# Storing two blocks to a transfer and asking for q and k two half-blocks sooner, in a fused attention and mixture-of-experts kernel

## The chip, the cores and the metric

The kernel runs on one core of a Trainium2 chip. The core has TensorE (PE, matrix products; PEld is its loading of weights), VectorE (DVE), ScalarE (ACT), GpSimd (POOL) and SyncE (SP), each with an instruction queue of its own that is worked through in order, and 16 DMA engines that all queues share. The metric is the device time of one execution in microseconds. The kernel before takes 1025.03 us (median of 3 runs, 1024.62 to 1025.8).

## The reference

Attention over 8 batches of 8 heads, 576 positions, head size 64, in a sliding window of 128 with a linear bias; its output, 4608 tokens by 512, goes through 8 experts that all tokens pass, weighted by a doubly normalised gate:

```python
scores = scale * np.matmul(q, k.transpose(0, 1, 3, 2))
scores = np.where(mask, scores + bias[None], -1000000000.0)
attn = softmax(scores)                       # written out in the reference
x = np.matmul(attn, v)  -> (4608, 512)
P = np.exp(x @ w_gate - max)
for _ in range(8):
    P /= P.sum(1, keepdims=True) + 1e-09
    P /= P.sum(0, keepdims=True) + 1e-09
    P *= N / E
for e in range(E):
    out += P[:, e:e + 1] * (np.maximum(x @ w1[e], 0.0) @ w2[e])
```

The gate P depends on sums over all tokens, so no expert's result can be weighted before the whole attention is done.

## The kernel before, in words

**Blocks and stages.** The tokens are 36 blocks of 128: four whole blocks of each batch (0 to 31), and the 64 last tokens of two batches together in each of blocks 32 to 35. The kernel has three stages: attention with experts 0 and 1 woven in (to about 285 us), the gate's eight rounds with the rest of experts 0 and 1 (to about 345 us), and experts 2 to 7 with a Strassen-like scheme (to the end).

**The attention loop.** `steps` goes over batch b, key block kb (0 to 4, the last one the 64-token tail) and half u of the heads; `at = 2 * kb + u` counts the ten half-blocks of a batch. A step does the scores and exponentials of the next half-block (`scores`, `exps`), its mask on VectorE (`masks`, L443), and the values product of this one (`values`, L468), whose normalised result VectorE writes into `xsb` (L479). Between them `filler.fill` puts in matmuls of experts 0 and 1 for blocks whose x is ready: `l1` (L115, ReLU on ScalarE L127) and `l2` (L137), whose result `psy` VectorE copies to a half-precision tile `yo` (`keep`, L555). `yo` is stored to DRAM (`ysp`, L541), since it can be weighted only after the gate. The order of blocks is 4 to 7 of expert 0, 0 to 3 of expert 1, 4 to 7 of expert 1, 8 to 11 of expert 0, 8 to 11 of expert 1, and so on. Blocks 0 to 3 of expert 0 go in one store of their own (L551).

**Buffers.** All PSUM products of this stage but the scores share four banks (`pmm`). `yo` is a ring of 6 tiles of one block, `xsb` one of 12, `a8` one of 8 large tiles for q, k, their casts `c16` and the turned `qk`. A tile that comes up again waits until its last use is over; for `yo` that is the landing of its store.

**SyncE's queue.** Every load, store and DMA transpose of the stage is issued by SyncE in the order in which the Python code emits it. `keep` calls `store(2)`, so that up to two older stores are held back and a block's store is emitted three copies later; `turn_x` likewise holds three of x's stores (`keep_x(3)`, L494). For batches from 3 on (`XPE = 3`) q and k go through: load (`load_qk`, L271), casts on VectorE and ScalarE (`cast_qk`, L287 and L289, at half-blocks 8, 9, 0 and 1), two DMA transposes (`turn_qk`, L301, at half-block 1), and a reordering on GpSimd for k and VectorE for q (`order_qk`, L312). x is turned by a DMA transpose too (`turn_x`, L519). At half-block 1 the tail of the next batch is loaded (`load_tail`, L260), and at every second half-block a block of v (`load_v`, L374). Where the step's calls stand:

```python
            if 1 <= b < B - 2 and at == 3:
                load_qk(b + 2)
            ...
                if at == 1:
                    turn_qk(b + 1)
                    order_qk(b + 1, 1, range(NDT))
```

**Last stage.** `yo`'s ring also serves the tiles `xtok`, `xs` and `s3` there; x is read back from `xd` and the results of experts 0 and 1 from `ysp`.

Of the kernel before, what the change touches and what calls it, by code (L numbers as in the profile page):

```python
# [14 lines left out]
def kernel(  # L15
# [10 lines left out]
    nc = tc.nc  # L26
# [137 lines left out]
            yield 0, a  # L164

    L1_US, L2_US = 0.87, 1.74
    XPE, YO, XSB = 3, 6, 12
    CAST_AT = ((0, 1, 2, 3), (1, 2, 3, 4))

    class Filler:  # L170
# [57 lines left out]
    sps = first_pool.enter_context(tc.tile_pool(name="sps", bufs=1, space=bass.MemoryType.PSUM))  # L228
    if True:
        mask = asb.tile([P, H, 2 * P], FP16, name="mask")  # L230
        rel = per.tile([P, HD], FP16, name="rel", tag="yo", bufs=YO)[:, 0 : 2 * P]

        def make_mask(ys):
            for y in ys:
# [80 lines left out]
                )  # L315

        def turn_tail(b):
            t16 = asb.tile([P, HD], FP16, name=f"t16_{b}", tag="xsb", bufs=XSB)
            nc.gpsimd.tensor_copy(out=t16, in_=tails.pop(b).rearrange("p h d -> p (h d)"))
            nc.sync.dma_start(out=QKT[b][2], in_=t16, transpose=True)  # L320

# [123 lines left out]
            )  # L445

        xsbs: dict = {}

        def values(b, kb, u):

            nk, _ = sizes(kb)
            if u == 0:
                xsbs[b, kb] = asb.tile([P, H, Dh], FP16, name=f"xsb_{b}_{kb}", tag="xsb", bufs=XSB)
            psN = aps.tile([P, GT], FP32, name=f"psN_{b}_{kb}_{u}", tag="pmm", bufs=4)
            if b == 0:
                spin(psN, 3)
            psN = psN[:, 0 : 4 * Dh + 4].rearrange("p (h d) -> p h d", h=4)
            ops = []
            for y in range(2):
                for hb in range(2):  # L460
                    hh = 2 * y + hb
                    if kb > 0:
                        ops.append((hh, pts[b, kb - 1, u][:, 2 * hb + y, P : P + nk], vs[b, kb - 1][:, 4 * u + hh, 0 : Dh + 1]))
                    ops.append((hh, pts[b, kb, u][0:nk, 2 * hb + y, 0:nk], vs[b, kb][0:nk, 4 * u + hh, 0 : Dh + 1]))
            if kb == NKB - 1:
                ops = ops[0::2] + ops[1::2]
            for i, (hh, lhsT, rhs) in enumerate(ops):
                nc.tensor.matmul(  # L468
                    out=psN[0:nk, hh, :],
                    lhsT=lhsT,  # L470
                    rhs=rhs,
                    start=(i == 0),
                    stop=(i == len(ops) - 1),
                )
# [15 lines left out]

        def keep_x(left=0):
            while len(kept) > left:
                blk, lo, nk, xsb = kept.pop(0)
                nc.sync.dma_start(out=xd[blk, lo : lo + nk, :], in_=xsb[0:nk].rearrange("p h d -> p (h d)"))  # L494

        def turn_x(b, kb):
            nk, _ = sizes(kb)
            blk = 4 * b + kb if kb < NKB - 1 else 4 * B + b // 2
            lo = 0 if kb < NKB - 1 else TL * (b % 2)
            xT, at = x_of(blk)  # L500
            to = xT[:, at, :, lo : lo + nk]
            xsb = xsbs.pop((b, kb))
            if by_pe(b):
                ps = aps.tile([P, NDT, P], FP16, name=f"psX_{b}_{kb}", tag="pmm", bufs=4)
                for j in range(NDT):
                    nc.tensor.matmul(
                        out=ps[:, j, 0:nk],
                        lhsT=xsb[0:nk, 2 * j : 2 * j + 2, :],
                        rhs=ident[0:nk, 0:nk],
                        is_transpose=True,  # L510
                        start=(j == 0),
                        stop=(j == NDT - 1),
                    )
                if b == 0:
                    nc.scalar.copy(out=to, in_=ps[:, :, 0:nk])
                else:
                    nc.vector.tensor_copy(out=to, in_=ps[:, :, 0:nk])  # L517
            else:
                nc.sync.dma_start(out=to, in_=xsb[0:nk].rearrange("p h d -> p (h d)"), transpose=True)  # L519
            kept.append((blk, lo, nk, xsb))  # L520
            keep_x(3)

        def gates(b0, b1):
            ps = aps.tile([P, b1 - b0, E], FP32, name=f"psG_{b0}", tag="pmm", bufs=4)
# [13 lines left out]
        def store(left=0):  # L538
            while len(stores) > left:
                e, blk, yo = stores.pop(0)  # L540
                nc.sync.dma_start(out=ysp[e, blk], in_=yo)  # L541

        first_y: list = []

        def keep(e, blk, ps):
            if blk < RI and e == 0:
                if not first_y:
                    first_y.append(per.tile([P, RI, HD], FP16, name="y_first", tag="a8", bufs=8))
                nc.vector.tensor_copy(out=first_y[0][:, blk, :], in_=ps)
                if blk == RI - 1:  # L550
                    nc.sync.dma_start(out=ysp[0, 0:RI].rearrange("m p d -> p m d"), in_=first_y[0])  # L551
                return
            store(2)
            yo = per.tile([P, HD], FP16, name=f"yo_{e}_{blk}", tag="yo", bufs=YO)
            nc.vector.tensor_copy(out=yo, in_=ps)  # L555
            stores.append((e, blk, yo))

        order = [(0, 0, 2), (0, 2, 2)]
        for b0 in range(RI, NBLK, 4):
# [129 lines left out]
        for n, (b, kb, u) in enumerate(steps):  # L689
# [72 lines left out]
                homes(1)  # L762
            if (b, at) == (1, 3):
                homes(2)
            if 1 <= b < B - 2 and at == 3:
                load_qk(b + 2)
            if XPE <= b + 1 < B - 1 and at >= 8:
                cast_qk(b + 2, at - 8)
# [113 lines left out]
        def scale_x(n):  # L882
            if n >= N:
                return
            g, e = units[n]
            for m in range(2):
                blk = 2 * g + m
                nc.scalar.mul(out=xs[2 * (n % 2) + m], in_=xtok[m], mul=P_sb[:, blk, e : e + 1])  # L888
            if e == E - 1 and n + 1 < N:
                if g == groups[0]:  # L890
                    xtok[:] = [per.tile([P, HD], FP16, name=f"xtok_{i}", tag="yo", bufs=YO) for i in range(2)]
                load_x(units[n + 1][0])

        def turn_xs(n):
# [19 lines left out]
        def quads_w1(e):  # L914
            w = W1L[e]
            q = dict(a11=w[:, 0:2, 0:HF], a12=w[:, 2:4, 0:HF], a21=w[:, 0:2, HF:Fd], a22=w[:, 2:4, HF:Fd])
            if e < E - 2:
                t = lp.tile([P, 3, 2, HF], FP16, name=f"s_{e}")
                q.update(s1=t[:, 0], s2=t[:, 1], s3=t[:, 2])
            elif e == E - 1:  # L920
                t = per.tile([P, 2, 2, HF], FP16, name=f"s_{e}", tag="xT", bufs=4)
                q.update(s1=t[:, 0], s2=t[:, 1])
                q["s3"] = [per.tile([P, HF], FP16, name=f"s3_{k}", tag="yo", bufs=YO) for k in range(2)]
            else:
                q.update((f"s{i}", aux[:, i].rearrange("p f n -> p (f n)").rearrange("p (k f) -> p k f", k=2)) for i in (1, 2, 3))
            q["s4"] = q["a21"]
            SL[e] = q

            def one(to, a, b, op):
                if isinstance(q[to], list):  # L930
                    for k in range(2):
                        nc.vector.tensor_tensor(out=q[to][k], in0=q[a][:, k], in1=q[b][:, k], op=op)
                else:
                    nc.vector.tensor_tensor(out=q[to], in0=q[a], in1=q[b], op=op)

            one("s1", "a21", "a22", ALU.add)
            one("s3", "a11", "a21", ALU.subtract)
            one("s2", "s1", "a11", ALU.subtract)
            one("s4", "a12", "s2", ALU.subtract)
# [28 lines left out]
        def part(n, ps, w, x, start=False):  # L968

            q = SL[units[n][1]][w]  # L970
            q = q if isinstance(q, list) else [q[:, k] for k in range(2)]
            for j in range(NF2):
                for k in range(2):
                    nc.tensor.matmul(  # L974
                        out=ps[:, j, :],
                        lhsT=q[k][:, P * j : P * j + P],
                        rhs=xset[n % 2][:, x, P * k : P * k + P],
                        start=(start and j == 0 and k == 0),
                        stop=(k == 1),
                        skip_group_check=True,  # L980
                    )
# [117 lines left out]
        s5 = s5y[:, 0].rearrange("p (f t) -> p f t", f=NF2)  # L1099
        y = s5y[:, 1].bitcast(FP16).rearrange("p (m d) -> p m d", m=2)  # L1100
        turn_xs(1)
        xs[:] = [per.tile([P, HD], FP16, name=f"xs_{i}", tag="yo", bufs=YO) for i in range(2)] * 2
        late: tuple = ()
        for n in range(N):
            g = units[n - 1][0]
# [103 lines left out]
```

## Time and profile before

| | |
|---|---|
| median of 3 runs | 1025.03 us (1024.62 to 1025.8) |
| profiled execution | 1025.63 us, span 1023.9 us |
| stores ysp<-yo | 68 of 128 KB, median 3.3 us to landing, 1.7 to 9.0 |
| stores xd<-xsb | 32 of 128 KB and 8 of 64 KB, median 3.2 us over both |
| q and k from batch 3 on | five loads each of 1024 KB, median 7.8 and 10.1 us |
| transposes qk<-c | ten, median 4.7 us |

Times on a timeline are microseconds from the span's start; a row gives start, duration, engine (SPq is SyncE's queue), line of the kernel, operation, output and inputs, count, and in brackets the idle time of the engine before it with what ended it. A transfer's row on SPq is the time that its issue held the queue; its landing is told apart from it.

### The profile page before, as it was taken

What the parts mean: (1) busy time and instruction counts of PE and PEld (TensorE: products, weight loads), DVE (VectorE), ACT (ScalarE), POOL (GpSimd) and SP (SyncE); (2) the same over time, 40 slices, a digit from 0 to 9 for tenths busy, and PEclk for the clock granted to TensorE, in tenths of its full rate; (3) what the DMA queues carried; (4) which work ended last, traced back from release to release, by engine and by line L of the source; (5) the groups of instructions that cost most, each with busy time, mean ns of one, the idle gap of its engine ahead of it and who ended that gap; (6) DMA issues with size and microseconds to landing.
All of it is one profiled execution on the core that took longest, in us unless ns stands there. A gap on an engine that the chain in (4) does not pass through costs nothing.

```text
span 1023.9 us, 27787 instructions
## 1 busy us (share of the span) xinstructions
PE 1000.3 (98%) x11487; PEld 801.6 (78%) x11487; DVE 749.5 (73%) x1594; ACT 722.2 (71%) x1240; POOL 78.8 (8%) x143
## 2 busy tenths in 40 slices
PE   7999999999999999999999999999999999999998
PEld 5645444444544698999999999999999999999997
DVE  5735665556578588877877877877887887787787
ACT  7646555555433457888888888888888888888885
POOL 1212033306110000000000000000000000000000
PEclk9999999999999999999999999999999999999999
DMA  9996689889999233343334334324334434333461
GB/s 244 219 271 170 143 221 220 191 196 180 221 192 177 69 72 80 71 81 94 74 64 100 76 66 94 73 64 94 77 65 98 81 71 81 86 82 65 98 115 47
DMA packets 264431, 122.46 MB, mean 120 GB/s; under 512 B 201968, under 2 KB 255728, under 8 KB 264304
## 3 DMA queue, kind: packets, MB, share of 16 engines
q1 hardware_dynamic: 249568, 102.68, 44.2%
q0 software_dynamic: 14304, 17.84, 10.5%
q8 instruction: 90, 1.47, 0.6%
q14 instruction: 37, 0.30, 0.1%
q10 hardware_dynamic: 432, 0.16, 0.1%
HBM read 78.30 MB, written 23.59 MB: 100 GB/s over the span
## 4 chain that ended last, share of the span: by engine, by line
PE 74%; DVE 3%; DMA 1%; ACT 1%; issue 0%; DVEq 0%; ACTq 0%; SPq 0%
PE psM L1011 30%; PE psB L974 13%; PE psA L974 9%; PE psC L974 9%; PE psy L137 5%; PE psh L115 5%; PE psh L953 2%; DVE acc L1055 1%; PE psN L468 1%; DMA acc<-xd 0%; DVE hs L1141 0%; PE psS L412 0%; DVE hs L991 0%; DVE hs L992 0%; DMA s5y<-ysp 0%
## 5 line engine op out<-in xcount | busy, mean ns | idle before, releaser
L1011 PEld LDWEIGHTS <-hs 128*128 128x128 f16 x2996 | 271.7, 98 | 22.4
L1011 PE MATMUL psM<-w2l,hs 128*128 128x256 f16 x1440 | 186.6, 273 | 0.0
L974 PEld LDWEIGHTS <-w1l 128*128 128x128 f16 x2720 | 173.2, 98 | 8.9 <-issue 3.0
L127 ACT ACTIVATE hT<-psh 128x512 f16<-128x512 f32 (+1 forms) x144 | 83.3, 586 | 100.9 <-PE psh L115 100.2
L987 ACT ACTIVATE hs<-hs 128x512 f16<-128x512 f16 x204 | 125.0, 630 | 34.3 <-DVE hs L1141 34.1
L1141 DVE TENSOR_TENSOR hs<-psB,s5y 128x512 f16<-128x512 f32 x102 | 70.4, 690 | 103.7 <-ACT xs L888 95.9
L115 PE MATMUL psh<-xT,w1t 128*128 128x512 f16 (+1 forms) x608 | 139.8, 368 | 3.2 <-DVE xT L517 2.4
L974 PEld LDWEIGHTS <-s 128*128 128x128 f16 x2040 | 135.3, 98 | 5.8
L888 ACT ACTIVATE xs<-xtok,L_sb 128x512 f16<-128x512 f16 x204 | 136.0, 720 | 0.6 <-DMA xset<-xs 0.6
L137 PE MATMUL psy<-w2t,hT 128*128 128x512 f16 x576 | 134.3, 379 | 0.0
L1011 PE MATMUL psM<-more,hs 128*128 128x256 f16 x864 | 129.0, 273 | 0.0
L974 PE MATMUL psA<-xset,w1l 128*128 128x128 f16 x1360 | 103.7, 219 | 0.0
L974 PE MATMUL psB<-xset,s 128*128 128x128 f16 x1360 | 103.7, 219 | 0.0
L137 PEld LDWEIGHTS <-hT 128*128 128x128 f16 x576 | 53.5, 98 | 60.9 <-issue 1.5
L555 DVE CAST yo<-psy 128x512 f16<-128x512 f32 x68 | 46.8, 690 | 72.1 <-PE psy L137 57.8
L115 PEld LDWEIGHTS <-w1t 128*128 128x128 f16 x608 | 54.7, 98 | 54.7 <-issue 7.0
L991 DVE TENSOR_TENSOR hs<-hs 128x1024 f16<-128x1024 f16 x107 | 74.0, 691 | 23.5 <-ACT hs L987 16.8
L430 ACT ACTIVATE pt<-psS 128x1024 f16<-128x1024 f32 (+2 forms) x80 | 67.7, 851 | 29.2 <-PE psS L412 22.7
L1135 ACT COPY psC<-psB 128x512 f32<-128x512 f32 x102 | 58.1, 570 | 36.5 <-PE psB L974 36.5
L1130 ACT COPY s5y<-psC 128x512 f32<-128x512 f32 x102 | 59.8, 586 | 25.5 <-PE psC L974 25.5
L443 DVE TENSOR_TENSOR pt<-pt,mask 128x1024 f16<-128x1024 f16 (+2 forms) x80 | 51.8, 647 | 32.8 <-ACT pt L430 32.7
L1055 DVE TENSOR_TENSOR acc<-acc,psM 128x256 f32<-128x256 f32 (+1 forms) x162 | 74.1, 503 | 2.1
(121 smaller groups left out, 1410.1 us busy)
## 6 DMA issues: line engine op xcount, KB each, us to landing
s5y<-ysp SPq DMA_DIRECT2D x36, 256.0 KB, 3.0
ysp<-yo SPq DMA_DIRECT2D x68, 128.0 KB, 3.3
v<-in_v_dram SPq DMA_DIRECT2D x32, 256.0 KB, 4.4
out_dram<-acc SPq DMA_DIRECT2D x31, 256.0 KB, 2.5
q<-in_q_dram SPq DMA_DIRECT2D x5, 1024.0 KB, 7.8
k<-in_k_dram SPq DMA_DIRECT2D x5, 1024.0 KB, 10.1
xtok<-xd SPq DMA_DIRECT2D x34, 128.0 KB, 2.3
w2t<-in_moe_w_dram POOLq DMA_DIRECT2D x4, 1024.0 KB, 10.9
```

The source lines that it names most:

```text
L115: nc.tensor.matmul(out=ps[:, 0:nt], lhsT=w1ts[e][:, dt, P * ft : P * ft + P], rhs=xT[:, at : at + nb, dt, :], start=(dt == 0), stop=(dt == ...
L127: nc.scalar.activation(out=st["hT"][:, ft, 0:nt], in_=ps[:, 0:nt], func=AF.Relu)
L137: nc.tensor.matmul(out=ps, lhsT=st["hT"][:, ft, P * ms : P * ms + P], rhs=w2ts[e][:, ft, :], start=(ft == 0), stop=(ft == NFT - 1),)
L430: nc.scalar.activation(out=pt[0:nk, :, 0 : nk + nn], in_=ps[0:nk, :, :, 0 : nk + nn].rearrange("p a y n -> p (a y) n"), func=AF.Exp, scale ...
L888: nc.scalar.mul(out=xs[2 * (n % 2) + m], in_=xtok[m], mul=P_sb[:, blk, e : e + 1])
L974: nc.tensor.matmul(out=ps[:, j, :], lhsT=q[k][:, P * j : P * j + P], rhs=xset[n % 2][:, x, P * k : P * k + P], start=(start and j == 0 and ...
L987: nc.scalar.activation(out=h[n][:, slot], in_=src, func=AF.Relu)
L991: nc.vector.tensor_tensor(out=t[:, 4:6], in0=t[:, 0:2], in1=t[:, 2:4], op=ALU.add)
L1011: nc.tensor.matmul(out=Ms[bk][:, half, :], lhsT=h[n][:, LEFT[m], f, :], rhs=W2L[e][RIGHT[m]][:, f, :], start=(e == 2 and f == 0 and half = ...
L1055: nc.vector.tensor_tensor(out=a, in0=a, in1=p2, op=op)
L1130: nc.scalar.copy(out=s5, in_=pc)
L1141: nc.vector.tensor_tensor(out=h[n][:, 3], in0=pb, in1=s5, op=ALU.add)
```

## The change

`yo` becomes a ring of 3 tiles of two blocks, `xsb` one of 6 tiles of two blocks, and a transfer to DRAM takes both blocks; the odd tail block of x still goes alone. A pair's store is emitted when the next pair is full (`store(1)` after the second copy). `load_qk(b + 2)` moves from half-block 3 to half-block 1 for b = 2 to 5, and there it stands in the code ahead of the casts and `turn_qk` of the same step. The tiles of the last stage that share the ring are cut from pairs, and the subtraction for s3 of the last expert is one instruction instead of two.

```diff
-    XPE, YO, XSB = 3, 6, 12
+    XPE, YO, XSB = 3, 3, 6
...
-            if u == 0:
-                xsbs[b, kb] = asb.tile([P, H, Dh], FP16, name=f"xsb_{b}_{kb}", tag="xsb", bufs=XSB)
+            if u == 0 and kb % 2 == 0:
+                pair = asb.tile([P, 2, H, Dh], FP16, name=f"xsb_{b}_{kb}", tag="xsb", bufs=XSB)
+                xsbs[b, kb], xsbs[b, kb + 1] = pair[:, 0], pair[:, 1]
+                pairs[b, kb] = pair
...
-                blk, lo, nk, xsb = kept.pop(0)
-                nc.sync.dma_start(out=xd[blk, lo : lo + nk, :], in_=xsb[0:nk].rearrange("p h d -> p (h d)"))
+                blk, lo, nk, n, pair = kept.pop(0)
+                nc.sync.dma_start(
+                    out=xd[blk : blk + n, lo : lo + nk, :].rearrange("m p d -> p m d"),
+                    in_=pair[0:nk, 0:n].rearrange("p m h d -> p m (h d)"),
+                )
...
-            kept.append((blk, lo, nk, xsb))
-            keep_x(3)
+            if kb % 2:
+                kept.append((blk - 1, lo, nk, 2, pairs.pop((b, kb - 1))))
+            elif kb == NKB - 1:
+                kept.append((blk, lo, nk, 1, pairs.pop((b, kb))))
+            keep_x(1)
...
-                nc.sync.dma_start(out=ysp[e, blk], in_=yo)
+                nc.sync.dma_start(out=ysp[e, blk : blk + 2].rearrange("m p d -> p m d"), in_=yo)
...
-            store(2)
-            yo = per.tile([P, HD], FP16, name=f"yo_{e}_{blk}", tag="yo", bufs=YO)
-            nc.vector.tensor_copy(out=yo, in_=ps)
-            stores.append((e, blk, yo))
+            if blk % 2 == 0:
+                yos.append(per.tile([P, 2, HD], FP16, name=f"yo_{e}_{blk}", tag="yo", bufs=YO))
+            yo = yos[-1]
+            nc.vector.tensor_copy(out=yo[:, blk % 2, :], in_=ps)
+            if blk % 2:
+                store(1)
+                stores.append((e, blk - 1, yo))
...
-            if 1 <= b < B - 2 and at == 3:
+            if 1 <= b < B - 2 and at == (3 if b == 1 else 1):
                 load_qk(b + 2)
...
-                q["s3"] = [per.tile([P, HF], FP16, name=f"s3_{k}", tag="yo", bufs=YO) for k in range(2)]
+                q["s3"] = per.tile([P, 2, HF], FP16, name="s3_e", tag="yo", bufs=YO)
```

More of the change, by code (lines that the diff above doesn't have):

```diff
@@ L230 @@
         mask = asb.tile([P, H, 2 * P], FP16, name="mask")
-        rel = per.tile([P, HD], FP16, name="rel", tag="yo", bufs=YO)[:, 0 : 2 * P]
+        rel = per.tile([P, 2, HD], FP16, name="rel", tag="yo", bufs=YO)[:, 0, 0 : 2 * P]
         def make_mask(ys):
@@ L317, in turn_tail @@
         def turn_tail(b):
-            t16 = asb.tile([P, HD], FP16, name=f"t16_{b}", tag="xsb", bufs=XSB)
+            t16 = asb.tile([P, 2, HD], FP16, name=f"t16_{b}", tag="xsb", bufs=XSB)[:, 0]
             nc.gpsimd.tensor_copy(out=t16, in_=tails.pop(b).rearrange("p h d -> p (h d)"))
@@ L447 @@
         xsbs: dict = {}
+        pairs: dict = {}
         def values(b, kb, u):
             nk, _ = sizes(kb)
-            if u == 0:
-                xsbs[b, kb] = asb.tile([P, H, Dh], FP16, name=f"xsb_{b}_{kb}", tag="xsb", bufs=XSB)
+            if u == 0 and kb % 2 == 0:
+                pair = asb.tile([P, 2, H, Dh], FP16, name=f"xsb_{b}_{kb}", tag="xsb", bufs=XSB)
+                xsbs[b, kb], xsbs[b, kb + 1] = pair[:, 0], pair[:, 1]
+                pairs[b, kb] = pair
             psN = aps.tile([P, GT], FP32, name=f"psN_{b}_{kb}_{u}", tag="pmm", bufs=4)
@@ L540, in store @@
                 e, blk, yo = stores.pop(0)
-                nc.sync.dma_start(out=ysp[e, blk], in_=yo)
+                nc.sync.dma_start(out=ysp[e, blk : blk + 2].rearrange("m p d -> p m d"), in_=yo)
         first_y: list = []
+        yos: list = []
         def keep(e, blk, ps):
@@ L890, in scale_x @@
                 if g == groups[0]:
-                    xtok[:] = [per.tile([P, HD], FP16, name=f"xtok_{i}", tag="yo", bufs=YO) for i in range(2)]
+                    t = per.tile([P, 2, HD], FP16, name="xtok", tag="yo", bufs=YO)
+                    xtok[:] = [t[:, 0], t[:, 1]]
                 load_x(units[n + 1][0])
@@ L929, in one @@
             def one(to, a, b, op):
[L930 to L934, printed above, removed]
+                nc.vector.tensor_tensor(out=q[to], in0=q[a], in1=q[b], op=op)
             one("s1", "a21", "a22", ALU.add)
@@ L970, in part @@
             q = SL[units[n][1]][w]
-            q = q if isinstance(q, list) else [q[:, k] for k in range(2)]
             for j in range(NF2):
@@ L975, in part @@
                         out=ps[:, j, :],
-                        lhsT=q[k][:, P * j : P * j + P],
+                        lhsT=q[:, k, P * j : P * j + P],
                         rhs=xset[n % 2][:, x, P * k : P * k + P],
@@ L1101 @@
         turn_xs(1)
-        xs[:] = [per.tile([P, HD], FP16, name=f"xs_{i}", tag="yo", bufs=YO) for i in range(2)] * 2
+        t = per.tile([P, 2, HD], FP16, name="xs", tag="yo", bufs=YO)
+        xs[:] = [t[:, 0], t[:, 1]] * 2
         late: tuple = ()
```

## The prediction

> **What bounds the kernel now.** I read the page first, then who waited for whom on TensorE, VectorE and ScalarE in the attention stage (75 to 350 us), then the timelines of SyncE, VectorE and TensorE round one batch.
>
> ```profile
> span 1023.9 us, 27787 instructions
> PE 1000.3 (98%) x11487; PEld 801.6 (78%) x11487; DVE 749.5 (73%) x1594; ACT 722.2 (71%) x1240; POOL 78.8 (8%) x143
> DMA  9996689889999233343334334324334434333461
> ```
>
> TensorE is the bound, and the DMA engines are nearly full for the first third only. The changed transfers lie there, so I look for TensorE's idle time there. The three next fences are waits from 75 to 350 us on TensorE and ScalarE, and from 60 to 345 on VectorE (total, times, longest).
>
> ```profile
> PE psN L468 <- DVE pt L443: 3.8, 4, 1.7
> PE psh L115 <- DVE xT L517: 1.4, 1, 1.4
> ```
> ```profile
> ACT c L289 <- DMA k<-in_k_dram: 14.7, 4, 7.3
> ```
> ```profile
> DVE yo L555 <- DMA ysp<-yo: 11.7, 5, 3.2
> ```
>
> TensorE's waits for VectorE sum to 5.2 us: no gain in this stage can be much more. Behind them stand two late transfers: k of the batch after next, for which ScalarE stood still 14.7 us, and stores of results, whose buffer a copy wants again, 11.7 us of VectorE. SyncE's queue in batch 3 (from 106.8 us on) shows why:
>
> ```profile
> 118.64 1.22 SPq L519 DMA_TRANSPOSE xT<-xsb  x1
> 119.92 1.42 SPq L494 DMA_DIRECT2D xd<-xsb  x1
> 121.39 0.42 SPq L374 DMA_DIRECT2D v<-in_v_dram  x1
> 121.91 6.18 SPq L301 DMA_TRANSPOSE qk<-c  x2
> 128.15 0.64 SPq L260 DMA_DIRECT2D t<-in_q_dram  x1
> 128.84 0.62 SPq L260 DMA_DIRECT2D t<-in_k_dram  x1
> 129.50 1.10 SPq L541 DMA_DIRECT2D ysp<-yo  x2
> ...
> 133.07 2.25 SPq L271 DMA_DIRECT2D q<-in_q_dram  x1
> 135.37 0.58 SPq L271 DMA_DIRECT2D k<-in_k_dram  x1
> 135.99 0.83 SPq L541 DMA_DIRECT2D ysp<-yo  x1
> ```
> ```profile
> q<-in_q_dram SPq DMA_DIRECT2D x1, 1024.0 KB, 7.7
> k<-in_k_dram SPq DMA_DIRECT2D x1, 1024.0 KB, 8.3
> ...
> ysp<-yo SPq DMA_DIRECT2D x1, 128.0 KB, 8.1
> ```
>
> The second fence has the landings of 133 to 137 us. k lands at 135.4 + 8.3 = 143.7 and the store issued behind it at 144.1, where such a store elsewhere takes 3.3 (median): what stands behind q and k in this queue lands after them. q to k took 10.6, 10.8 and 10.7 us in batches 3, 4 and 5. VectorE and TensorE at the two places that matter:
>
> ```profile
> 121.27 0.69 DVE L555 CAST yo<-psy 128x512 f16<-128x512 f32 x1 [0.70 <-PE psy L137]
> ...
> 125.85 0.69 DVE L555 CAST yo<-psy 128x512 f16<-128x512 f32 x1 [0.63 <-PE psy L137]
> ...
> 126.56 0.68 DVE L443 TENSOR_TENSOR pt<-pt,mask 128x1024 f16<-128x1024 f16 x1
> ...
> 144.16 0.69 DVE L555 CAST yo<-psy 128x512 f16<-128x512 f32 x1 [2.89 <-DMA ysp<-yo]
> ```
> ```profile
> 130.30 0.41 PE L468 MATMUL psN<-v,pt 128*128 128x65 f16 x8
> ```
>
> At 144.16 a copy stands until the store issued at 135.99 has landed; TensorE lost 1.7 us behind it and behind ScalarE's wait for k. The copies at 121.27 and 125.85 are blocks 9 and 10 of expert 0 (the copies counted in the program's order). The mask of 126.56 is what the values matmul of 130.30 needs.
>
> **What the change does, part by part.**
>
> *Fewer transfers.* 68 stores of results become 34, 40 of x become 24, so 50 issues go at 0.43 (ysp) and 0.58 us (xd): about 24 us of SyncE's time, which no one waits for except through a late transfer. Bytes stay. From 250 us on these stores are followed by nothing that the queue holds them for, and a copy comes 10 us and more after its buffer's store has landed; there the pairs cost nothing. A pair lands 256 KB; the nearest rows, `out` at 2.5 and `ysp` at 3.3 us, bound it, and I take 3. By the Trainium skill (DMA: Bandwidth & Descriptors, "Anatomy of one DMA") a transfer costs a fixed 2 us plus its bytes at 436 GB/s, which makes a pair 0.3 us later than a single; its fit is for the other kind of queue, and the sum would change by that 0.3 us at each wait below.
>
> *The rings of buffers.* Six singles become three pairs. Before, the store of a block was put in the queue three copies later and was due three copies after that. Now pair n goes into the queue after the second copy of pair n+1, and the first copy of pair n+3 waits for it: one pair's time is left, not counting what stands between in the queue. That is the step that I expect to cost. x's pairs (six of two for twelve) are reused a batch and a half later, long landed. In the last part the two subtractions for s3 become one, once, on VectorE beside TensorE: nothing.
>
> *q and k sooner.* In the built program of the changed kernel q and k now stand ahead of the transposes qk<-c of the same step, two half-blocks (6.5 to 11 us) sooner. ScalarE's and VectorE's waits for them go. But the transposes, the tail loads and the next store of results now stand behind 2 MB.
>
> *Batch 2* (gain). q and k move into a stretch where SyncE sits idle (76.9 to 85.9 us), so what stood behind them lands sooner; the 1.4 us (psh waiting for xT at 108 us, behind ScalarE's wait for k) go: -1.4, at worst 0.
>
> *Batch 3* (the main cost). The new order is xT, v, q, k, qk<-c twice, t twice, then the store of blocks 4 and 5 of expert 1, for which the copy of block 10 of expert 0 (125.85) waits. xT still waits for xsb, so q is issued at 118.64 + 1.22 + 0.5 = 120.4. k lands 10.6 later, 131.0. The transposes then need their own turn: two of them landed 2.5 us apart in batches 4 to 6, so 136. From the second transpose's landing to that of the store behind the tail loads took 2.3 us (batches 4 and 5): 138.3. The copy is held from 125.85 to 138.3, 12.4 us of VectorE, and in VectorE's queue behind it stand the logits' copy and the mask. The mask ended 1.4 us after the copy began (125.85 to 127.24), so now at 139.7; TensorE, which reached that matmul at 130.30, waits 9.4 us. What it can do till then without VectorE, it has done by 130.30. Less the 0.5 us that it waited at 132.1 anyway: +9. Lower bound: the transfers pass beside q and k and the store lands at 132.5 as now; then the mask is done at 133.9: +3.1 with that gap taken off. Upper: 139.5 with SyncE itself held up, +10.1. I take 9, because the row behind q and k at 135.99 shows the full delay.
>
> *End of batch 3.* The copy at 144.16 (block 10 of expert 1, ready at 141.3) then needs the pair (0: 8, 9), which stands behind xT<-xsb of the last full block (xsb done 140.64), xd, v: 140.6 + 1.2 + 0.6 + 0.5 + 2.5 and its issue = 145.5 on the old clock, against 144.07. That wait does not go, it changes its cause: +1.1 (0 to 1.5).
>
> *Batches 4 and 5.* The same step, but the copy that waits comes later (block 14 of expert 0, 163.91, for pair (1: 8, 9)). xT<-xsb at 150.0, q at 151.8, k lands 162.4, transposes 164.9 and 167.4, then t, xT, xd, v (4 us of issue from 165) and the store at 168.8: landed 171.7, 7.8 us of VectorE. TensorE has filler matmuls and one free PSUM bank until about 169 to 170, and the copy frees its bank at 172.4: +3 (0 if the transposes pass; 4.5 if the mask behind the copy is needed too). Later in these batches the second copy of a pair no longer waits (181.99, 2.07 us): TensorE's 1.3 us at 183 and 0.3 at 217 go. Batch 4: +1.7. Batch 5: +2.7.
>
> *Batch 6* loads no q or k; the store due at 233.4 lands near 237, TensorE loses 0.5 (0 to 1.5).
>
> Sum: -1.4 + 9 + 1.1 + 1.7 + 2.7 + 0.5 = +13.6 us. The profiled execution took 1025.63 (span 1023.9 and 1.7 round it), 0.6 over the median of the runs, 1025.03. So 1039.2 on its own time, and 1038.6 as a median.
>
> **Rivals.**
>
> *Relief* (faster). If pair stores land before the next pair's copy, the 50 issues less and the early q and k take the late transfers away: all of the 5.2 us go, 1025.0 - 5.2 = 1019.8, down to 1022 if half stays. For it: every one of the five store waits lies right behind a q and k load or in the backlog after one. Against it: the store that batch 3 needs is issued, even now, at 129.50, 3.6 us after the copy that will wait for it; it decides if the store lands before 128.9, which is 130.30 less the 1.4 us to the mask's end. The Trainium skill speaks for this case (DMA: Bandwidth & Descriptors, "Rules for kernel authors"): many small transfers are to be coalesced into one large one. No wait in this trace is for SyncE's issue time alone.
>
> *Transfers pass.* The wait in batch 3 is real, but the transposes and stores share the engines with q and k: +3.1 in batch 3, nothing in 4 to 6, the gains -1.4, -1.3, -0.3: 1025.1, up to 1030 where they pass only in part. Against it the 144.1 above.
>
> *Late transposes bite further.* kN (POOL) starts after the second transpose, now 5 to 6 us later, ahead of v's and the tail's casts, for which tT and the stores behind it wait in SyncE's queue: 4.5 in each of batches 4 and 5, 1 more at each one's end, 10.1 + 1.5 in batch 3, 1.5 in batch 6, no gains: +24.1, 1049.
>
> **How the numbers follow.** The main case 0.62 (own range 1031 to 1046), relief 0.13, transfers pass 0.16, the further bite 0.09. Within 0.2% (2 us, about what a measurement of this kernel can tell from no change) lies half of the third case: same 0.08. Faster 0.13, slower 0.62 + 0.08 + 0.09 = 0.79. The range 1025 to 1046 leaves out relief (0.13) and most of the last case (0.07).
>
> **What would show it.** Right: in waits, DVE yo L566 <- DMA ysp<-yo grows from 11.7 to 25 us and more, one of them near 12 in batch 3 round 126 to 138; TensorE's wait for the mask grows from 1.7 to about 9 there; ACT c <- DMA k is gone; qk<-c lands 8 us and more after issue. Wrong: that copy runs without a wait, because q and k drain faster than 10.6 us, or the transposes land beside them. Past 350 us both traces should differ by a constant.

## The result and the profile after

The changed kernel takes 1051.73 us (median of 4 runs, 1051.13 to 1053.71), the kernel before 1024.82 us in runs beside it: a ratio of 1.0264, 95% interval 1.0247 to 1.028, slower by 26.9 us. The profiled execution took 1051.13 us, 25.5 more than that of before. The first lines of its page, with the granted clock of the 40 slices (before: 9 in all of them):

```profile
span 1049.4 us, 27689 instructions
...
PE 1009.3 (96%) x11487; PEld 805.3 (77%) x11487; DVE 746.9 (71%) x1593; ACT 722.5 (69%) x1240; POOL 75.7 (7%) x143
...
PEclk8999989989999999999999999999999999999999
```

The same number of matmuls takes 9 us more of busy time, and TensorE stands idle longer: two losses, not one. The waits of TensorE (75 to 350 us) and VectorE (60 to 345 us), as total, times, longest:

```profile
PE psN L471 <- DVE yo L566: 15.2, 3, 6.9
PE psy L137 <- DVE yo L566: 2.2, 1, 2.2
PE psN L471 <- DVE pt L443: 2.2, 3, 1.2
PE psh L115 <- DVE xT L523: 1.4, 1, 1.4
```
```profile
DVE yo L566 <- DMA ysp<-yo: 34.3, 4, 12.3
```

VectorE's waits for stores grew from 11.7 to 34.3 us, and TensorE now waits behind the waiting copy. ScalarE's wait for k is gone after 75 us. SyncE's queue in batch 3, then VectorE and TensorE there:

```profile
120.99 1.23 SPq L525 DMA_TRANSPOSE xT<-xsb  x1
122.27 0.58 SPq L374 DMA_DIRECT2D v<-in_v_dram  x1
122.90 0.83 SPq L271 DMA_DIRECT2D q<-in_q_dram  x1
123.78 0.66 SPq L271 DMA_DIRECT2D k<-in_k_dram  x1
124.53 10.32 SPq L301 DMA_TRANSPOSE qk<-c  x2
134.90 1.01 SPq L260 DMA_DIRECT2D t<-in_q_dram  x1
135.97 0.63 SPq L260 DMA_DIRECT2D t<-in_k_dram  x1
136.64 0.62 SPq L550 DMA_DIRECT2D ysp<-yo  x1
```
```profile
126.32 0.69 DVE L443 TENSOR_TENSOR pt<-pt,mask 128x1024 f16<-128x1024 f16 x1 [0.87 <-ACT pt L430]
...
139.86 0.69 DVE L566 CAST yo<-psy 128x512 f16<-128x512 f32 x1 [12.29 <-DMA ysp<-yo]
...
140.56 1.41 DVE L443 TENSOR_TENSOR pt<-pt,mask 128x1024 f16<-128x1024 f16 x1
```
```profile
131.82 1.89 PE L137 MATMUL psy<-w2t,hT 128*128 128x512 f16 x8 [0.24 <-ACT hT L127]
140.60 0.21 PE L471 MATMUL psN<-v,pt 128*128 128x65 f16 x1 [6.89 <-DVE yo L566]
142.03 0.57 PE L471 MATMUL psN<-v,pt 128*128 128x65 f16 x7 [1.22 <-DVE pt L443]
...
144.55 3.60 PE L115 MATMUL psh<-xT,w1t 128*128 128x512 f16 x8
```

The order, the long issue and the late store are the ones forecast: the store is issued at 136.64, lands at 139.7, and the copy starts at 139.86. The last line is what the forecast did not have: eight matmuls take 3.60 us. Their row in the kernel before:

```profile
132.32 1.89 PE L115 MATMUL psh<-xT,w1t 128*128 128x512 f16 x8
```

The clock says why. Stretches of the kernel after: length, busy time of PE, PEld, DVE, ACT and POOL, then the granted clock, the DMA share and GB/s:

```profile
137.80:148.00 10.20, 6.18 (x28) 2.48 (x27) 6.54 (x14) 2.00 (x3) 6.20 (x9) 0.50 0.70 124
148.00:158.00 10.00, 10.00 (x77) 4.93 (x77) 6.33 (x16) 5.19 (x9) 1.32 (x4) 1.00 0.50 118
185.60:189.00 3.40, 3.40 (x10) 1.03 (x7) 3.33 (x9) 1.46 (x3) 0.51 (x2) 0.50 0.26 87
223.10:229.90 6.80, 4.40 (x17) 1.73 (x17) 5.47 (x12) 0.77 (x2) 2.81 (x8) 0.50 0.50 130
```

After each of the three long stalls TensorE runs at half of its clock. In batches 4 and 5 the stall and the slow matmuls behind it are these, the first row being that of twelve such matmuls in the kernel before:

```profile
168.86 2.75 PE L115 MATMUL psh<-xT,w1t 128*128 128x512 f16 x12
```
```profile
184.15 0.19 PE L471 MATMUL psN<-v,pt 128*128 128x65 f16 x1 [3.72 <-DVE yo L566]
...
184.85 4.44 PE L115 MATMUL psh<-xT,w1t 128*128 128x512 f16 x12
```
```profile
224.82 0.21 PE L471 MATMUL psN<-v,pt 128*128 128x65 f16 x1 [4.60 <-DVE yo L566]
...
226.09 4.65 PE L115 MATMUL psh<-xT,w1t 128*128 128x512 f16 x12
```

### The profile page after: what moved, and what is told of

It is laid out like the page before. It is cut to its first block, busy times and chain, and to the rows that moved or that the text cites. A ratio compares the mean times of both kernels' runs of the same rounds, so it can differ in the third digit from the quotient of the medians.

```text
span 1049.4 us, 27689 instructions
## 1 busy us (share of the span) xinstructions
PE 1009.3 (96%) x11487; PEld 805.3 (77%) x11487; DVE 746.9 (71%) x1593; ACT 722.5 (69%) x1240; POOL 75.7 (7%) x143
## 3 DMA queue, kind: packets, MB, share of 16 engines
q0 software_dynamic: 14304, 17.84, 10.2%
## 4 chain that ended last, share of the span: by engine, by line
PE 85%; DVE 5%; issue 4%; DMA 4%; SPq 1%; ACT 1%; POOL 0%; DVEq 0%; POOLq 0%; ACTq 0%
PE psM L1020 30%; PE psB L983 13%; PE psh L115 10%; PE psy L137 9%; PE psA L983 8%; PE psC L983 8%; PE psh L963 2%; DMA ysp<-yo 1%; PE psN L471 1%; PE psS L412 1%; DMA v<-in_v_dram 1%; DVE pt L443 1%; PE psT L351 1%; SPq L301 1%; DMA k<-in_k_dram 1%
## 5 line engine op out<-in xcount | busy, mean ns | idle before, releaser
L115 PE MATMUL psh<-xT,w1t 128*128 128x512 f16 (+1 forms) x608 | 145.8, 380 | 3.3 <-DVE xT L523 2.4
L137 PE MATMUL psy<-w2t,hT 128*128 128x512 f16 x576 | 134.3, 379 | 2.4 <-DVE yo L566 2.2
L983 PEld LDWEIGHTS <-s 128*128 128x128 f16 x1904 | 126.3, 98 | 5.6 <-issue 0.2
L983 PE MATMUL psB<-xset,s 128*128 128x128 f16 x1224 | 93.3, 219 | 0.0
## 6 DMA issues: line engine op xcount, KB each, us to landing
w2t<-in_moe_w_dram POOLq DMA_DIRECT2D x4, 1024.0 KB, 11.1
```

The costliest lines, as they stand in the source:

```text
L115: nc.tensor.matmul(out=ps[:, 0:nt], lhsT=w1ts[e][:, dt, P * ft : P * ft + P], rhs=xT[:, at : at + nb, dt, :], start=(dt == 0), stop=(dt == ...
L137: nc.tensor.matmul(out=ps, lhsT=st["hT"][:, ft, P * ms : P * ms + P], rhs=w2ts[e][:, ft, :], start=(ft == 0), stop=(ft == NFT - 1),)
L983: nc.tensor.matmul(out=ps[:, j, :], lhsT=q[:, k, P * j : P * j + P], rhs=xset[n % 2][:, x, P * k : P * k + P], start=(start and j == 0 and ...
```

## The experiments

Each kernel has runs of the kernel before on its own chip, and its ratio is to those. Four shared the first chip (pairs only, early only, four pairs, stored at once), four the second (TensorE kept busy, four pairs late, four pairs behind, at once behind), and eight singles, singles behind and the two repeats the third. The last column goes by one profiled execution of each kernel.

| kernel | ring of results | q, k at half-block | median us | ratio, 95% interval | VectorE's waits for stores in the profile, us (longest) |
|---|---|---|---|---|---|
| before | 6 singles | 3 | 1024.82 | 1 | 11.7 (3.2) |
| changed | 3 pairs | 1, ahead of the transposes | 1051.73 | 1.0264, 1.0247 to 1.028 | 34.3 (12.3) |
| pairs only | 3 pairs | 3 | 1049.75 | 1.0225, 1.0195 to 1.0254 | 37.9 (11.1) |
| early only | 6 singles | 1, ahead | 1034.96 | 1.009, 1.0067 to 1.0114 | 12.2 (5.0) |
| four pairs | 4 pairs | 1, ahead | 1026.85 | 1.0016, 0.9995 to 1.0037 | 2.2 |
| stored at once | 3 pairs | 1, ahead | 1032.32 | 1.0062, 1.0045 to 1.0079 | none |
| TensorE kept busy | 3 pairs | 1, ahead | 1045.5 | 1.0202, 1.0156 to 1.0248 | 30.6 in batches 3 to 5 (12.9) |
| four pairs, late | 4 pairs | 3 | 1021.23 | 0.9971, 0.9953 to 0.9989 | 4.9 (1.9) |
| four pairs, behind | 4 pairs | 1, behind the transposes | 1025.53 | 0.9998, 0.9978 to 1.0019 | 7.4 (2.8) |
| at once, behind | 3 pairs | 1, behind | 1025.51 | 1.0005, 0.9983 to 1.0027 | none |
| eight singles | 8 singles | 3 | 1023.37 | 0.9973, 0.9956 to 0.999 | none |
| singles, behind | 6 singles | 1, behind | 1034.39 | 1.0092, 1.0076 to 1.0108 | 15.6 (7.0) |

### Each half alone

The changed kernel with q and k back at half-block 3:

```diff
-            if 1 <= b < B - 2 and at == (3 if b == 1 else 1):
+            if 1 <= b < B - 2 and at == 3:
```

> The pairs alone: q and k are asked for at half-block 3 as in the kernel before; all else is the changed kernel. Theory (a pair has one pair's time of slack, and what stands ahead of its store in SyncE's queue decides when it lands): in batch 3 the store of blocks 4 and 5 of expert 1 then follows the tail loads with no q and k ahead of it, so it is issued near 129.5 and lands near 132.5; the copy of block 10 of expert 0 is held about 7 us instead of 12.3. In batches 4 and 5 the waited pair now stands right behind q and k and lands near 12 us after the copy is ready, so VectorE is held about 12 us instead of 8.7 and 9.6. VectorE's waits for stores stay near 30 us in sum; 1038 to 1048. Rival (q and k ahead of the transposes is the whole cause): 1023 to 1027, waits for stores back near 12.

Measured 1049.75: the pairs alone cost nearly all of it, a little over the range given. Batch 3 went as the theory said (held 5.9 us instead of 12.3), batches 4 and 5 too: there the waited store stands right behind q and k, issued at 172.94 and landed at 183.4, where the store after it took 3.0.

```profile
171.16 0.64 SPq L271 DMA_DIRECT2D q<-in_q_dram  x1
171.85 1.05 SPq L271 DMA_DIRECT2D k<-in_k_dram  x1
172.94 1.78 SPq L550 DMA_DIRECT2D ysp<-yo  x1
```
```profile
183.55 0.69 DVE L566 CAST yo<-psy 128x512 f16<-128x512 f32 x1 [11.15 <-DMA ysp<-yo]
```

So the stores are late behind q and k at either place; moving them only changes the batch in which it hurts. The rival, that the place of q and k is the whole cause, falls.

The other half alone, the kernel before with this one line changed:

```diff
-            if 1 <= b < B - 2 and at == 3:
+            if 1 <= b < B - 2 and at == (3 if b == 1 else 1):
```

> The earlier q and k alone: the kernel before with its single-block transfers and rings of six and twelve, with q and k asked for at half-block 1 in batches 2 to 5. Theory: a single's store has three copies of slack, so the later transposes and stores are hidden; ScalarE's wait for k (14.7 us) goes and VectorE's waits for stores stay under 15 us: 1020 to 1027. Rival (transposes and the reordering behind 2 MB are what costs, whatever the rings): 1035 or more, with the same long VectorE wait near 126 to 138.

Measured 1034.96 (1029.92 to 1038.63 over nine runs): the theory missed. The 12 us wait of batch 3 is indeed not there, and VectorE's waits for stores stay at 12.2 us. But TensorE has a wait that neither profile had shown, for the scores of batch 4:

```profile
PE psN L468 <- DVE pt L443: 3.2, 2, 1.9
PE psS L412 <- DVE qN L312: 1.9, 2, 1.0
```

qN is VectorE's reordering of the transposed q. Its last copies stand behind a copy of results that is held for a store, and they take 2.52 us, where those of the kernel before at 138.03 took 1.17. GpSimd copies kN beside them: it had waited for k's transpose until 135.98, and in the kernel before it was done with kN at 134.3. So the late store and the late transposes both have a part in the wait:

```profile
137.77 0.69 DVE L555 CAST yo<-psy 128x512 f16<-128x512 f32 x1 [2.56 <-DMA ysp<-yo]
138.38 2.52 DVE L312 COPY qN<-qk 128x512 f16<-128x512 f16 x2
```

In batches 4 and 5 a copy still waits 4.6 and 5.0 us for a store behind the transposes, so three copies of slack run out too, by less. The profiled execution was the shortest of the nine, so the same kernel was profiled again:

> The earlier q and k alone in single blocks, once more, since its profiled execution (1029.9 us) was the shortest of its nine and stood 5 us under their median. Theory (the same stalls, but more of them followed by a stretch at half of the clock): store waits near 12 us again, and two to four more half-speed stretches of 3.4 us where the time is above 1031. Rival (a stall that the first profile did not have): a new wait of 2 us or more.

This one took 1033.11 us. The store waits are 10.8 us, as expected, in two of 6.0 and 4.8. From 75 us on there is no new wait of 2 us, but ahead of that there is one, for GpSimd's v, where the first profile had a wait of 0.96 us:

```profile
40.38 0.54 PE L468 MATMUL psN<-v,pt 128*128 128x65 f16 x7 [2.63 <-POOL v L385]
```

A half-speed stretch goes with it (3.4 us, from 39.8 on), and by 50 us this execution is 2.8 us behind the first one. That is the rival's new stall, and most of the 3.2 us between the two, at a place that the moved request does not touch. The only other half-speed stretch is at 395 us, so the theory's stretches behind the store stalls are not shown. Where the longest of the nine lost their time stays open.

### More time for a store

The changed kernel with a fourth pair (2 KB more in each partition, which the weight tile frees):

```diff
-    XPE, YO, XSB = 3, 3, 6
+    XPE, YO, XSB = 3, 4, 6
...
-        F1_6 = lp.tile([P, NF2, HB], FP16, name="f1_6")
...
+        F1_6 = per.tile([P, 2, HD], FP16, name="f1_6", tag="yo", bufs=YO).rearrange("p a (b n) -> p (a b) n", b=2)
```

> The changed kernel with a ring of four pairs of results instead of three; for room one weight tile of the last stage is taken from that ring. The order of SyncE's queue is the changed kernel's. Theory: with two pairs of time the store that lands at 139.8 is wanted only about two copies later, so the 12 us wait shrinks to under 3 us, and with it TensorE's stalls and its half-speed stretches: 1019 to 1028. Rival (SyncE's queue itself, its late transposes, tail loads and x stores cost the time, not the ring): 1035 or more with no long wait for a store.

Measured 1026.85, as the theory said. SyncE's queue is as held up as before (the two transposes hold it 11.93 us from 127.95), but nobody waits for the store any more: one wait of 2.2 us. So the ring decides 25 of the 27 us. (The profiled execution, 1031.81, is the slowest of the ten; two of its three half-speed stretches, at 10.0 and 44.4, lie ahead of the first moved request.) What is left in this stage is the scores of batch 4 again, behind a transpose that VectorE waits 2.0 us for and the 2.2 us of the store, and their wait is followed by a half-speed stretch (146.8 to 150.2):

```profile
145.83 0.28 PE L412 MATMUL psS<-qN,kN 64*128 64x256 f16 x2 [1.23 <-DVE qN L312]
147.13 0.40 PE L412 MATMUL psS<-qN,kN 64*128 64x256 f16 x2 [1.02 <-DVE qN L312]
```

The same without more room, by storing a pair as soon as it is full:

```diff
             if blk % 2:
-                store(1)
                 stores.append((e, blk - 1, yo))
+                store(0)
```

> The changed kernel with three pairs, but a pair's store goes into the queue as soon as its second copy is issued, not when the next pair is full. In batch 3 the store of blocks 4 and 5 of expert 1 then stands ahead of q, k and the transposes. Theory: a store gets one pair more of time, the long waits of VectorE go (in sum under 12 us) and TensorE's stalls and half-speed stretches with them: 1018 to 1027. Rival (a store put into the queue sooner holds SyncE until its copy has run, so x's transposes behind it come late, and the time is lost there): 1030 to 1045, with waits for xT in place of those for stores.

Measured 1032.32, inside the rival's range and 5 us over the theory's. No copy waits for a store at all, which bears out the theory's mechanism, and the rival's waits for xT are not there (xT is 0.4 us longer). The profiled execution is 6.4 us longer than that of before. By the starts of the exponentials it loses 2.9 us round 41 us, behind a 2.62 us wait for GpSimd's v, and 3.5 us between 104 and 113 on the clock of before, both ahead of batch 3's stall; the scores of batch 4 wait 1.0 us for kN. Three half-speed stretches of 3.4 us, at 41.5, 113.2 and 147.3, stand in it, where before has none. Whether the other nine executions lost their time there is not shown. At once, with q and k behind the transposes:

```diff
-            if 1 <= b < B - 2 and at == (3 if b == 1 else 1):
+            if b == 1 and at == 3:
                 load_qk(b + 2)
...
                 load_tail(b + 1)
+            if 1 < b < B - 2 and at == 1:
+                load_qk(b + 2)
```

> Three pairs as in the changed kernel, a pair's store put into the queue as soon as its second copy is issued, and q and k asked for behind the transposes and the tail loads of half-block 1. Theory (place in the queue is all; the 128 KB per partition row of a fourth pair is not needed): no store wait over 3 us, the scores of batch 4 not late: 1019 to 1025. Rival (the store of a pair then stands right behind q and k and one pair's time is too little): 1030 or more with store waits of 5 us and longer.

(The row of a fourth pair is 2 KB per partition, not the figure in that text.) Measured 1025.51, half a microsecond over the range and 6 us less than stored at once, by the ratios: no store wait, and TensorE waits 0.2 us for qN. The store order and the place of q and k together undo the loss with the changed kernel's buffers. (Stored at once with q and k left at half-block 3 was not run.)

### The clock behind a stall

Matmuls that no one reads, in TensorE's idle time ahead of the three long stalls:

```diff
             ps = st["psy"]
+            if e == 0:
+                spin(ps, {11: 60, 15: 32, 19: 42}.get(blk, 0))
```

> The changed kernel with matmuls that nobody reads added on TensorE in blocks 11, 15 and 19 of expert 0 (60, 32 and 42 of them, into the bank that the block's product then overwrites): they run while TensorE would stand still for the long store waits of batches 3, 4 and 5. Theory (a stall costs twice: its own length, and the stretch at half of the clock behind it): VectorE's waits for stores stay at 30 us or more, the granted clock stays at 1.0 round 138 to 148, 185 to 189 and 223 to 230, and the time falls by 6 to 8 us, to 1043 to 1046. Rival (the matmuls after a stall are slow because of late operands, not of the clock): 1050 to 1053, or later by what the added matmuls take.

Measured 1045.5 by median; the profiled execution, 1042.34, is the shortest of the four. The added matmuls fill the wait, which ends no earlier for VectorE, and those behind it run at the full clock:

```profile
128.68 6.71 PE L251 MATMUL psy<-ones 128*128 128x256 f16 x60 [0.24 <-ACT hT L127]
...
138.05 0.19 PE L473 MATMUL psN<-v,pt 128*128 128x65 f16 x1 [0.93 <-DVE yo L568]
...
141.05 1.89 PE L115 MATMUL psh<-xT,w1t 128*128 128x512 f16 x8
```
```profile
137.31 0.69 DVE L568 CAST yo<-psy 128x512 f16<-128x512 f32 x1 [12.88 <-DMA ysp<-yo]
```
```profile
137.80:148.00 10.20, 8.64 (x68) 4.06 (x67) 8.17 (x21) 4.23 (x8) 5.12 (x9) 1.00 0.52 133
```

VectorE stands still ahead of the three copies for 12.9, 8.3 and 9.4 us (12.3, 8.7, 9.6 in the changed kernel), the eight matmuls take 1.89 instead of 3.60, and the granted clock is 1.0 until the end. (The store of batch 4 landed at 177.6 and that of batch 5 at 216.8, 0.1 us ahead of the copies, though the waits are booked there to matmuls for the scores, which these copies do not read.) A kernel with more work is 6 us shorter by the ratios, whose intervals just touch; the rows show that the slow stretch belongs to the clock and is a second price of a stall. The Trainium skill states this (TensorE: Matmul & The Clock Gate, "Part 1: The HAM clock gate"): the clock falls to half after an idle window of about 3.4 us and comes back after one that is busy, and the windows run on regardless of the kernel. The trace agrees: stretches of 10.2, 3.4 and 6.8 us at 0.5.

### A version that beats both

Four pairs, with q and k at half-block 3:

> Four pairs of results, and q and k asked for at half-block 3 as in the kernel before. Theory (with two pairs of time no store is late, and what was left of the loss with four pairs, near 3 us round 138 to 150 us, came from q and k standing ahead of the transposes): VectorE's waits for stores under 4 us, the scores of batch 4 wait for no qN, ScalarE's wait for k is back near 14 us: 1020 to 1025. Rival (pairs themselves cost, by waits for x or for the backlog behind 256 KB): 1027 or more.

Measured 1021.23, faster than the kernel before by 0.3%. VectorE's waits for stores, 4.9 us, are a little more than expected, and ScalarE's for k, 9.8 us, less. No wait for qN is left, and a store behind k may land 10 us after its issue (132.36 to 142.5) at a price of 1.87 us on VectorE:

```profile
131.56 0.76 SPq L271 DMA_DIRECT2D k<-in_k_dram  x1
132.36 1.32 SPq L550 DMA_DIRECT2D ysp<-yo  x1
```
```profile
142.55 0.69 DVE L566 CAST yo<-psy 128x512 f16<-128x512 f32 x1 [1.87 <-DMA ysp<-yo]
```

In more runs, on another chip:

> Four pairs of results, q and k at half-block 3, in more rounds. Theory: a ratio to the kernel before of 0.995 to 0.999, with a granted clock of 1.0 through the attention stage. Rival (the gain was one chip's chance): 0.999 to 1.003.

Measured 1022.17, ratio 0.997 (0.9957 to 0.9984), with the clock at 1.0 from 4.9 to 1018.7 us. The gain stands.

Is it the pairs? The kernel before with two single tiles more, the same bytes as four pairs:

```diff
-    XPE, YO, XSB = 3, 6, 12
+    XPE, YO, XSB = 3, 8, 12
...
-        F1_6 = lp.tile([P, NF2, HB], FP16, name="f1_6")
...
+        F1_6 = [
+            per.tile([P, HD], FP16, name=f"f1_6_{k}", tag="yo", bufs=YO).rearrange("p (f n) -> p f n", f=2)
+            for k in range(2)
+        ]
```

> The kernel before with its single-block transfers and q and k at half-block 3, but a ring of eight singles of results: the same bytes as four pairs. (One weight tile of the last stage is cut from the ring, and one subtraction there is two instructions.) Theory (only the time that a store is given counts, not how many blocks a transfer holds): the 11.7 us of store waits of the kernel before go, and the time is that of four pairs at half-block 3, 1019 to 1024. Rival (the gain of four pairs comes from the 50 transfers fewer in SyncE's queue): as the kernel before, 1023 to 1027, store waits of 5 us or more left.

Measured 1023.37, a ratio of 0.9973: the same gain, without one transfer less. VectorE waits for no store. So depth pays, and at this depth pairing by itself neither pays nor costs. In the prediction a rule of the Trainium skill (DMA: Bandwidth & Descriptors, "Rules for kernel authors": coalesce many small transfers) spoke for the change; no run here shows a gain from it.

And four pairs with the early request behind the transposes:

> Four pairs of results, and q and k asked for at half-block 1, but behind the transposes and the tail loads of that step. Theory: the transposes land as in the kernel before, so the scores of batch 4 are not late, q and k are still in time for ScalarE, and the stores behind them have two pairs of time: 1018 to 1023, the fastest of these. Rival (what stands behind q and k is then xT and the stores, and TensorE waits for xT instead): 1026 to 1035.

Measured 1025.53, no change, 2.5 us over the range. From batch 3 on its profile runs as that of four pairs late (3.3 and 3.1 us gained on the kernel before), though the scores of batch 4 do wait 0.67 us for qN, behind a copy held 2.80 us for a store. It had lost 5.2 us ahead of that, with half-speed stretches at 39.7 and 111.3; the first goes with a 2.63 us wait for GpSimd's v and lies ahead of any moved request. The rival's waits for xT are not in it. Why the median of ten executions is 4 us over that of four pairs late is not shown by one profile. Singles with the early request behind:

```diff
-            if 1 <= b < B - 2 and at == 3:
+            if b == 1 and at == 3:
                 load_qk(b + 2)
...
+            if 1 < b < B - 2 and at == 1:
+                load_qk(b + 2)
```

> The kernel before with its rings of single blocks, q and k asked for at half-block 1 but behind the transposes and the tail loads of that step. Theory (the earlier request alone cost 9 us because transposes and stores then stood behind 2 MB): with the transposes ahead of it the scores of batch 4 are not late, and the stores behind q and k wait at most as in the kernel before: 1021 to 1027. Rival (any 2 MB at half-block 1 costs, wherever it stands in the step): 1031 to 1037.

Measured 1034.39, as the rival said. With the transposes ahead the stores are late instead, and the scores of batch 4 are late all the same, because the copies of qN stand behind a copy that is held for a store:

```profile
143.65 0.69 DVE L555 CAST yo<-psy 128x512 f16<-128x512 f32 x1 [4.06 <-DMA ysp<-yo]
```
```profile
144.99 0.71 PE L412 MATMUL psS<-qN,kN 64*128 64x256 f16 x4 [1.94 <-DVE qN L312]
```

In batch 4 the store behind k is issued at 168.01 and lands at 177.3:

```profile
167.39 0.58 SPq L271 DMA_DIRECT2D k<-in_k_dram  x1
168.01 1.95 SPq L541 DMA_DIRECT2D ysp<-yo  x1
```
```profile
177.43 0.69 DVE L555 CAST yo<-psy 128x512 f16<-128x512 f32 x1 [6.96 <-DMA ysp<-yo]
```

With six singles some copy is late wherever in this half-block the 2 MB stand, ahead or behind; with four pairs, or with three that are stored at once, none waits more than 2.8 us.

## Why the prediction was wrong

The direction, the place and the mechanism of the wait were right; the time, 1038.6, was 13 us short and its range ended at 1046. The step that failed is the price of a stall: the sum took TensorE's stalls at their length and put the clock behind them at nothing, which is 6.5 us here. It also took the stalls of batches 4 to 6 too short and counted a gain in batch 2 that did not come. The start of each step's exponentials on ScalarE is compared with that of the same step before (us later, over stretches between steps, rounded). The kernel with TensorE kept busy gives the stalls without the half clock.

| stretch | forecast | changed kernel | TensorE kept busy |
|---|---|---|---|
| to half-block 6 of batch 2 | 0 | +2.3 | -1.1 |
| to half-block 6 of batch 3 | -1.4 | +0.6 | +0.9 |
| to half-block 2 of batch 4 | 9 + 1.1 = +10.1 | +8.8 | +6.7 |
| to half-block 2 of batch 5 | +3 | +6.0 | +4.2 |
| to half-block 2 of batch 6 | -1.3 + 3 = +1.7 | +6.2 | +3.9 |
| to the end of the stage | -0.3 + 0.5 = +0.2 | +1.9 | +1.5 |
| sum | +13.6 | +25.7 | +16.1 |

The changed kernel exceeds the forecast by 12.1 us: 2.3 at the start, 2.0 to half-block 6 of batch 3, and 7.8 in the four rows behind it, 6.5 of them the clock.

**The missing term: the clock.** The sum priced a stall of TensorE at its length. In the traces it is followed by 3.4 to 10.2 us at 0.5. The third to sixth rows differ by 2.1, 1.8, 2.3 and 0.3 us between the last two columns: 6.5 us. The long rows say the same: 3.60 for 1.89, 4.44 for 2.75, 4.65 for 2.75 are 5.3 us, and more in the shorter rows beside them. The rule stood in the Trainium skill and was not weighed; every row of before had the clock at 1.0.

**The main cost (batch 3).** VectorE was forecast to be held 12.4 us, and the row at 139.86 has 12.29. That row counts from the end of VectorE's work before; from 128.16 on, when the copy's product was ready, the copy is held 11.7 us. The store landed 0.9 us sooner than forecast (137.4 on the old clock, that is in the times of the kernel before, 2.35 us less here, for 138.3), but the mask behind the copy took 1.41 us instead of 0.68, so TensorE went on at 139.7 on the old clock, as forecast: two misses that nearly cancel. It waited 6.89 + 1.22 = 8.1 us instead of 9.4, because it came to that matmul 0.9 us later, after waits of 0.44 and 0.24 us for ScalarE's hT that the kernel before does not have. That the end of batch 3 would cost 1.1 was wrong: the shift falls by 2.2 us behind the stall, because the waits of before round 144 us, VectorE's for the store and ScalarE's for k, are not there any more.

**Batches 4, 5 and 6 were too small.** TensorE stood 4.0 (3.72 and 0.28), 5.3 and 2.2 us against 3, 3 and 0.5. In batch 4 the store was right (landed at 183.3; 171.6 on the old clock, forecast 171.7), but TensorE had stopped at 180.43, 168.8 on the old clock, not "until about 169 to 170", and waited a little for the mask behind the copy too. In batch 6 the held copy starts at 260.20, 236.8 on the old clock (forecast: a store landing near 237), but TensorE had less to do till then than assumed.

**The gain in batch 2 did not come.** The 1.4 us of psh for xT are in the changed kernel and in every other one, whether ScalarE waits for k or not. On VectorE of the kernel before, xT's copy stands in a row of work without a gap since 101.11, so the step that named ScalarE's wait for k as its cause was wrong:

```profile
107.84 0.40 DVE L517 COPY xT<-psX 128x512 f16<-128x512 f16 x1
```

**The start.** 2.3 us were lost ahead of batch 1 to late first loads and a half-speed stretch (8.1 to 14.9). The four other kernels with rings of three pairs are between 1.4 us earlier and 0.2 us later than before at the end of batch 0, so it is not put down to the change.

**The rivals.** Relief and transfers that pass beside q and k are refuted by the rows at 124.53 and 136.64. The late transposes that bite further gave 1049, the nearest number, for another reason: GpSimd does wait 81 us in all for qk<-c, for 26 before, but TensorE of the changed kernel waits for no qN or kN, since the store holds it longer. With that store out of the way a bite comes out at the scores of batch 4: 1.9 us in early only and 2.3 in four pairs, where a shorter store wait on VectorE has its part in it, and 1.0 us in stored at once, which has no store wait. The two halves do not add up: by the ratios 23 us of the pairs and 9 of the earlier request make 27.

**Two readings.** By the sum's own rows q and k move 12.7 and 13.0 us (133.07 to 120.4 and 164.75 to 151.8), not "6.5 to 11"; the times in the sum are the right ones, with q issued at 120.5 on the old clock in batch 3. The median of 3.2 us given for the stores of x counts x's transposes too; the forty stores alone have 3.6 us, and no sum uses it.

## What to carry to other kernels

Two blocks to a transfer in the same bytes halve the number of slots: count, for the copy that reuses a slot, what was put in the store's queue ahead of it and how long that takes to land, before counting the transfers saved. Two megabytes moved earlier in SyncE's queue made something behind them late, ahead of the transposes as well as behind them; the depth of the ring and the order of the stores decided whether anyone waited. Price a long stall of TensorE at its length and add the half-speed stretch behind it (3.4 to 10.2 us here).

## What the hardware showed

The clock fell to half after less than 3.4 us of unbroken idleness: with four pairs, two waits of 1.23 and 1.02 us with short matmuls between them (143.7 to 147.5) were followed by 0.5 from 146.8 to 150.2, while a single wait of 1.4 us at 108 us in the kernel before was not, nor one of 2.20 us at 260.94 in the changed kernel. The records at 0.5 last 3.41 us or two or three times that. In three profiles (early only taken again, stored at once, four pairs behind) a stretch near 40 us goes with a TensorE wait of 2.6 us for GpSimd's v; the kernel before waits 0.96 us at that place and has none. Near 111 us the waits do not decide it: singles behind has a stretch after a wait of 1.38 us for xT, and at once behind has none after 1.77. What decides there was not tried.

Two DMA transposes that took 6.18 us of SyncE's time in batch 3 of the kernel before took 9.53 to 11.93 in the kernels that put 2 MB ahead of them: not only does the transfer land late, SyncE itself is held in the issue. In the changed kernel the first of the two holds it for 8.25 us, until 132.8, and k lands at 133.0 (123.78 + 9.2).
